# Group 7's second MLP product in seven products of quarters, two slices behind, with its activations' sums on GpSimd

## The chip, the cores and the metric

The kernel runs on one core of one Trainium2 chip. The metric is the device time of one execution in microseconds; lower is better. The kernel before takes 924.25 us (median of three runs, 924.24 to 924.6).

The engines are TensorE (PE; PEld is its weight load), VectorE (DVE), ScalarE (ACT), GpSimd (POOL) and SyncE (SP, which here issues DMAs). Each serves its own list of instructions and waits for the others by semaphores.

## What is computed

Two steps, one after the other. Windowed causal attention with a linear bias over 8 batches of 8 heads, 576 positions, head dimension 64; then a SiLU MLP over the 4608 tokens of width 512, with 2048 hidden features:

```python
scores = where(0 <= i - j < 128, q @ k.T / 8 - slope[h] * (i - j), -1e9)
x = softmax(scores) @ v                       # 4608 tokens x 512
h = x @ w_in                                  # 4608 x 2048
out = (h / (1 + exp(-h))) @ w_out             # 4608 x 512
```

## The kernel before

The tokens are worked through in nine groups of 512 (`NG`, group 0 to 8). A group's MLP is made in 16 slices (`NF`); slice n = 16 g + f has a first product (`gemm1`), an activation in four steps and a second product (`gemm2`). While group g's MLP runs, the attention of group g + 1 is worked through beside it, one pair p (a block of 128 queries, half of the heads) every eight positions of a plan.

**Numbers.** From group 2 on, the operands of the MLP are float16 in two parts, high and low. A product of two such operands is three matmuls: high by high, high by low, low by high.

**Ordinary groups.** `gemm1` makes 12 matmuls of 512 columns into one PSUM bank (tag "h", two banks). `act1` (ACT, L752) is the Tanh of it, `act2` (DVE, L761) turns this into the activation, `act3` (ACT, L778) makes its high part `gh`, `act4` (DVE, L795) its low part `gl`. `gemm2` (L908) makes 12 matmuls of 512 columns, three for each of four token tiles, which gather over the 16 slices in the four banks w, x, y, z. `store` (L929) reads them out.

**The groups in `FAST`** (L67), only the last one before. There a slice is 256 tokens by two tiles of features, and a group falls into two units t = 0, 1 of 256 tokens and eight slices each. `gemm1_fast` (L697) makes 24 matmuls of 256 columns. The second product, a 2x2 by 2x2 product of blocks, is made from seven products of sums of blocks (M1 to M7, Strassen's) instead of eight plain ones: 7 x 3 = 21 matmuls of 256 columns in `gemm2_fast` (L825). For that the activation has seven blocks of 128 instead of four; `act_sums` (L769) makes three of them new by sums, two instructions of 256 elements and one of 128. `act3` and `act4` then each take 640 and 256 elements in two instructions. The sums of the weights are made earlier by GpSimd and ACT (`SUM_WORK`, from position 332 on; the group before the last begins at position 448). M1 has bank z, M5 and M2 bank x, M3 and M4 bank w, M7 and M6 bank y. At the end of a unit `join_products` (L878) adds the seven results up: after the first half of the last slice's second product ACT copies bank x into `once` and DVE reads M1; after the second half DVE reads bank w as a whole, M4 and M3 singly, then bank y; `store_fast` (L872) sends the four quarters out. The last slice of all (`LAST`, 143) is made plainly by `gemm2_last` (L851), in four pieces of six matmuls.

**The order of the work** is written out by hand. The loop over groups makes a list `seq` of halves: two of a slice's first product and two of an earlier slice's second product (`behind`). Each entry is a position; `begin()` (L1161) first issues what the plan has for this position, sorted by `rank` (normalize first, then act2, act_sums, act3, act4, then row_max, p_lo and their kind, then the rest), and then the half product is issued; `act1` follows the second half of a first product. `put` sets plan entries by absolute position, `ahead` by distance from the present one. For a pair whose scores are at position n, in the last batches: `hi16` n-10 and n-8 (ACT), `lo16` n-6 and n-5 (DVE), `scores` n (TensorE), `row_max` n+1 (DVE, four times 256 elements), `exps` n+2 and n+3 (ACT, two each), `p_hi` n+3 and n+4 (ACT), `p_lo` and the DMA transposes n+4 and n+5 (DVE, SP), `attend` n+12 (TensorE), `normalize` n+13 (DVE), `x_hi` and `x_lo` n+15 (ACT, DVE). A new block of values adds `v_hi` at n+7, on GpSimd or, when the group at this position is in `FAST`, on ACT (L421), and `v_lo` at n+8 (DVE). Scores and attended values share two PSUM banks tagged "a" in turn.

In ordinary groups, as group 7 was, slice n-1's second product follows slice n's first, and `act3` and `act4` come two positions after `act1`. In the last group the second products skip slices 1 and 9, to be made up in slices 2 and 10, and those of the last three slices come together at the end.

Waits are set by the tiles: a new tile in a ring of buffers waits for the readers of the tile that had its place.

Of the kernel before, what the change touches and what calls it, by code (L numbers as in the profile page):

```python
# [6 lines left out]
F32 = mybir.dt.float32  # L7
# [10 lines left out]
P = 128  # L18
# [45 lines left out]
Q16 = ("w1_2", "w1_3")  # L64
K16 = ("w1_4", "w1_5", "w1_6")
CUT = 2.0**-25
FAST = (NG - 1,)  # L67
HALF_F = NF // 2
SUMS, SUMS_STEP = 332, 14
SUM_TAGS = tuple(f"w1_{k}" for k in range(7, 15))  # L70
MORE_TAGS = (("w1_15", 1), ("k", KSLOTS), ("k", KSLOTS))
# [25 lines left out]
def tile_window_attention_then_silu_mlp(ctx, tc, qk, qk16, v, w_in, w_out, distance, out):  # L97
# [60 lines left out]
    def ps_of(tag, name):  # L158
        t = psum.tile([P, DM], F32, tag=tag, bufs=2 if tag in "ah" else 1, name=name)
        if tag == "a":  # L160
            spare["a"] = t
        return t
# [615 lines left out]
    def act3(n):  # L778
        gt = gact[n]
        if n // NF in FAST:  # L780
            gh, gl = (pool.tile([P, 7, P], F16, tag=tag, name=f"{tag}{n}") for tag in ("gh", "gl"))
            gact[n] = (gh, gl, gt)
            for to, of in parts_of(n):
                nc.scalar.activation(gh[:, to], gt[:, of], AF.Copy, scale=0.5 * CUT)
            return
        dt = F32R if n // NF < OUT16 else F16
        gh = pool.tile([P, TG], dt, tag="gh", name=f"gh{n}")
        gl = pool.tile([P, TG], dt, tag="gl", name=f"gl{n}")
        if n // NF < OUT16:
            (nc.vector.tensor_copy if at_edge(n) else nc.scalar.copy)(gh, gt)  # L790
        else:
            nc.scalar.activation(gh, gt, AF.Copy, scale=CUT)  # L792
        gact[n] = (gh, gl, gt)
# [31 lines left out]
    def gemm2_fast(n, half):  # L825
        g, (t, j) = n // NF, divmod(n % NF, HALF_F)
        last = LAST - 1 if n // HALF_F == LAST // HALF_F else n - j + HALF_F - 1
        if n == LAST:
            gemm2_last(half)
            return  # L830
        gh, gl, _ = gact[n]
        products = (M5, M2, M1, M3) if half == 0 else (M4, M7, M6)
        for a, parts in ((gh, (0, 1)), (gl, (0,))):
            for k in products:
                b, side = PLACE[k]
                if j == 0 and side == 0 and a is gh:
                    ops[b] = psum.tile([P, DM], F32, tag="wxyz"[b], name=f"m{g}_{t}_{b}")
                for part in parts:
                    nc.tensor.matmul(  # L839
                        product(k), a[:, k], sum_part(k, j, part),  # L840
                        start=j == 0 and side == 0 and a is gh and part == 0, stop=n == last and a is gl,
                        skip_group_check=True,
                    )
        if n == last:
            join_products(g, t, half)

    def product(k):
        b, side = PLACE[k]
        return ops[b][:, side * (DM // 2) : (side + 1) * (DM // 2)]

    def gemm2_last(half):  # L851

        gh, gl, _ = gact[LAST]
        if half == 0:
            ops["c"] = ps_of("a", "last")
        c = ops["c"][:, half * (DM // 2) : (half + 1) * (DM // 2)]
        for col, o in ((0, product(M7)), (1, c)) if half == 0 else ((0, c), (1, product(M6))):
            seq = [
                (a[:, k], w16[1, HALF_F - 1 + far * HALF_F][:, part, col * (DM // 2) : (col + 1) * (DM // 2)])
                for k, far in ((2 + half, 0), (half, 1)) for a, part in ((gh, 0), (gh, 1), (gl, 0))  # L860
            ]
            for i, (lhs, rhs) in enumerate(seq):
                nc.tensor.matmul(
                    o, lhs, rhs, start=half == 0 and col == 1 and i == 0, stop=i == len(seq) - 1, skip_group_check=True
                )
            add_product(o, st["out"][0 if half == col else 1][:, half], NG - 1)
            store_fast(NG - 1, 1, half, col)

    def add_product(m, o, g):
        nc.vector.scalar_tensor_tensor(out=o, in0=m, scalar=gsc[g][:, 2:3], in1=o, op0=ALU.mult, op1=ALU.add)  # L870

    def store_fast(g, t, row, col):  # L872

        first = g * TG + (2 * t + row) * P
        rows = out[first : first + P, col * (DM // 2) : (col + 1) * (DM // 2)]
        (nc.scalar if row and col else nc.sync).dma_start(rows, st["out"][0 if row == col else 1][:, row])

    def join_products(g, t, half):  # L878

        scale = gsc[g][:, 2:3]  # L880
        if half == 0:
            st["out"] = [pool.tile([P, 2, DM // 2], F32, tag="q", bufs=2, name=f"of{g}_{t}_{k}") for k in range(2)]
            st["once"] = once = pool.tile([P, 2, DM // 2], F32, tag="io", name=f"once{g}_{t}")
            nc.scalar.activation(once.rearrange("p a c -> p (a c)"), ops[1], AF.Copy, scale=scale)
            for k in range(2):
                nc.vector.scalar_tensor_tensor(
                    out=st["out"][0][:, k], in0=product(M1), scalar=scale, in1=once[:, k], op0=ALU.mult, op1=ALU.subtract
                )
            return
        (corner, other), once = st["out"], st["once"]  # L890
        nc.vector.scalar_tensor_tensor(
            out=other, in0=ops[0].rearrange("p (a c) -> p a c", a=2), scalar=scale, in1=once, op0=ALU.mult, op1=ALU.add
        )
        for k, m in enumerate((M4, M3)):
            add_product(product(m), corner[:, k], g)
        if n_last(g, t):
            return
        nc.vector.scalar_tensor_tensor(
            out=corner, in0=ops[2].rearrange("p (a c) -> p a c", a=2), scalar=scale, in1=corner, op0=ALU.mult, op1=ALU.add
        )  # L900
        for row in range(2):
            for col in range(2):
                store_fast(g, t, row, col)

    def n_last(g, t):
        return g == NG - 1 and t == 1
# [130 lines left out]
    def put(point, fn, *a):  # L1037
        plan.setdefault(max(point, at(0)), []).append((fn, a))
# [78 lines left out]
    for g in range(1, NG):  # L1117
        put(max(8, at(2 * GT * g) + 10), x_unit, g)
        if g >= IN16:
            put(g * SLICE * NF - 2, mlp_scales, g)  # L1120
    for b in range(1, NBB):

        n = at(2 * GT * (NBLK * b // GT)) + 2
# [14 lines left out]
    def ahead(n, fn, *a):  # L1138
        plan.setdefault(pos[0] + n, []).insert(0, (fn, a))
# [26 lines left out]
    with tc.manual_schedule():  # L1166
# [37 lines left out]
            pos[0] += 1  # L1204
        bank.update(scores=[("a", "a")])

        for g in range(NG):
            now[0] = g

            seq = []  # L1210
            for f in range(NF):
                n = g * NF + f
                behind = [n - 1] if f or g - 1 in FAST else []
                if g in FAST and f in (1, 2, HALF_F + 1, HALF_F + 2):
                    behind = [] if f % HALF_F == 1 else [n - 2, n - 1]
                if g == NG - 1 and f >= NF - 2:
                    behind = [] if f == NF - 2 else [n - 2, n - 1, n]
                elif f == NF - 1 and g not in FAST:
                    behind += [n]
                seq += [("g1", n, 0), ("g1", n, 1)]  # L1220
                seq += [("g2", k, half) for k in behind for half in range(2)]
            for k, n, half in seq:
                begin()
                x_send()
                if k == "g1":
                    gemm1(n, half)
                    if half == 1:
                        act1(n)
                        if n % NF == NF - 1:
                            turn_over(n)  # L1230
                        elif n // NF in FAST and n // NF < NG - 1:
                            ahead(4, act4, n)
                            ahead(3, act3, n)
                            ahead(1, act_sums, n)
                            ahead(1, act2, n)
                        else:
                            late = 1 if n == 0 else 2
                            ahead(3 if 0 < n < NF else late, act4, n)
                            ahead(late, act3, n)
                            ahead(1, act2, n)  # L1240
                else:
                    gemm2(n, half)
                    if n % NF == NF - 1 and n // NF not in FAST:
                        store(g, 2 * half)
                        store(g, 2 * half + 1)
                if g == 0 and (pos[0] in TAKE or pos[0] > TAKE[-1] and pos[0] % 2 == 0):
                    w_next()
                pos[0] += 1
# [41 lines left out]
```

## Time and profile before

| | us |
|---|---|
| median of three runs | 924.25 |
| profiled execution, its own time | 924.52 |
| its span, first to last instruction | 922.7 |
| first Tanh of group 7 | 747.0 |
| first Tanh of group 8 | 840.5 |
| TensorE busy in the span | 910.3 |
| VectorE busy in the span | 697.9 |
| ScalarE busy in the span | 579.0 |
| GpSimd busy in the span | 203.9 |

The profile is of one execution, taken by the hardware profiler. Lines such as L732 are lines of the kernel above. A row of the grouped view has line, engine, operation, what is written and read, shape, count, then busy time and mean duration in ns, then the engine's idle time before these instructions and what ended it. A row of the timeline has start, duration, engine, line, operation, names, shape and how many instructions are merged in it; in brackets the idle time before it and its releaser. A row of the stages has the stretch, its length, the busy times of PE, PEld, DVE, ACT and POOL with counts, the granted TensorE clock and the DMA's share. TensorE's matmuls are pipelined, their ends are modelled, and GpSimd's spans are rough; the spacing of starts is firmer than a duration.

### The profile page before, as it was taken

What the parts mean: (1) busy time and instruction counts of PE and PEld (TensorE: products, weight loads), DVE (VectorE), ACT (ScalarE), POOL (GpSimd) and SP (SyncE); (2) the same over time, 40 slices, a digit from 0 to 9 for tenths busy, and PEclk for the clock granted to TensorE, in tenths of its full rate; (3) what the DMA queues carried; (4) which work ended last, traced back from release to release, by engine and by line L of the source; (5) the groups of instructions that cost most, each with busy time, mean ns of one, the idle gap of its engine ahead of it and who ended that gap; (6) DMA issues with size and microseconds to landing.
All of it is one profiled execution on the core that took longest, in us unless ns stands there. A gap on an engine that the chain in (4) does not pass through costs nothing.

```text
span 922.7 us, 17992 instructions
## 1 busy us (share of the span) xinstructions
PE 910.3 (99%) x6765; PEld 604.5 (66%) x6765; DVE 697.9 (76%) x1704; ACT 579.0 (63%) x1195; POOL 203.9 (22%) x195
## 2 busy tenths in 40 slices
PE   9999999999999999999999999999999999999997
PEld 7867777777787887555555555545455555547886
DVE  6889876446777778898788879888888876645665
ACT  7778997675456764666677756666766665533332
POOL 2343442222221220000000003455655200000000
PEclk9999999999999999999999999999999999999999
DMA  8977825243376645434698736444554464311000
GB/s 303 402 184 223 255 60 134 69 92 73 77 214 155 173 123 136 105 100 104 118 250 209 212 95 160 115 104 104 160 114 108 113 161 103 78 35 59 1 24 23
DMA packets 198182, 122.94 MB, mean 133 GB/s; under 512 B 166480, under 2 KB 167632, under 8 KB 198096
## 3 DMA queue, kind: packets, MB, share of 16 engines
q1 hardware_dynamic: 197664, 121.41, 49.9%
q8 instruction: 53, 0.87, 0.4%
q10 hardware_dynamic: 432, 0.39, 0.2%
q14 instruction: 33, 0.27, 0.1%
HBM read 71.96 MB, written 9.44 MB: 88 GB/s over the span
## 4 chain that ended last, share of the span: by engine, by line
PE 82%; DVE 6%; ACT 2%; issue 1%; ACTq 0%; DVEq 0%
PE o L924 33%; PE h L732 24%; PE h L737 8%; PE av L554 4%; PE h L704 4%; PE sp L450 3%; PE m L839 3%; PE sp L457 2%; DVE gt L763 1%; DVE hr L504 1%; DVE t L480 0%; ACT t L490 0%; DVE w L1021 0%; DVE vmx L209 0%; ACT gt L759 0%
## 5 line engine op out<-in xcount | busy, mean ns | idle before, releaser
L924 PE MATMUL o<-w,gh 128*128 128x512 f16 (+1 forms) x1024 | 313.2, 387 | 0.0
L732 PE MATMUL h<-xt,w 128*128 128x512 f16 (+1 forms) x1344 | 266.7, 349 | 0.0
L924 PE MATMUL o<-w,gl 128*128 128x512 f16 (+1 forms) x512 | 197.3, 385 | 0.3 <-DVE gl L147 0.2
L759 ACT ACTIVATE gt<-h,gsc 128x512 f32<-128x512 f32 x112 | 76.9, 686 | 186.1 <-PE h L732 164.6
L732 PEld LDWEIGHTS <-w 128*128 128x128 f16 x1344 | 125.7, 98 | 103.2 <-issue 2.2
L763 DVE SCALAR_TENSOR_TENSOR gt<-gt,h 128x512 f32<-128x512 f32 x144 | 98.4, 683 | 89.3 <-ACT gt L759 88.3
L490 ACT ACTIVATE t<-t,mx 128x256 f32<-128x256 f32 (+1 forms) x288 | 125.8, 486 | 6.0 <-DVE mx L480 5.7
L504 DVE SCALAR_TENSOR_TENSOR hr<-t,hr 128x512 f16<-128x512 f32 (+1 forms) x128 | 96.7, 761 | 30.1 <-ACT hr L499 30.0
L924 PEld LDWEIGHTS <-gh 128*128 128x128 f16 x640 | 62.1, 98 | 74.3 <-ACT gh L792 0.3
L737 PE MATMUL h<-xh,w 128*128 128x512 f32 x256 | 89.8, 405 | 0.0
L426 POOL TENSOR_SCALAR v<-rv,vsc 128x512 f16<-128x512 f32 x30 | 27.5, 917 | 277.2 <-DMA rv<-v 204.2
L804 DVE SCALAR_TENSOR_TENSOR gl<-gt,gh 128x512 f16<-128x512 f32 x80 | 62.0, 775 | 33.8 <-ACT gh L792 32.7
L924 PEld LDWEIGHTS o<-w,gh 128*128 128x128 f32 x384 | 69.8, 188 | 15.3 <-DVE vsc L269 0.3
L145 POOL TENSOR_TENSOR gl<-gt,gh 128x512 fp32r<-128x512 f32 x30 | 38.6, 1286 | 164.1 <-ACT gh L790 148.8
L499 ACT ACTIVATE hr<-t 128x512 f16<-128x512 f32 (+1 forms) x128 | 71.7, 595 | 1.4 <-DVE hr L504 1.4
L792 ACT ACTIVATE gh<-gt 128x512 f16<-128x512 f32 x80 | 50.3, 629 | 25.3 <-DVE gt L763 22.6
L554 PEld LDWEIGHTS <-hl 128*128 128x128 f16 x1464 | 51.4, 98 | 16.5 <-issue 5.2
L480 DVE CUSTOM_DVE_ANT_0 t<-sp,tab,vsc 128x256 f32<-128x256 f32 (+1 forms) x144 | 58.5, 460 | 1.1 <-PE sp L450 0.7
L924 PEld LDWEIGHTS <-gl 128*128 128x128 f16 x320 | 31.3, 98 | 38.6 <-DVE gl L804 1.0
L554 PE MATMUL av<-v,hl 128*128 128x65 f16 (+1 forms) x1464 | 54.8, 193 | 1.6 <-DVE mx L480 1.5
L145 POOL TENSOR_TENSOR w<-wm,w 128x512 fp32r<-128x512 f32 x32 | 43.4, 1358 | 58.6 <-ACT w L981 58.3
L737 PEld LDWEIGHTS h<-xh,w 128*128 128x128 f32 x256 | 48.1, 188 | 12.2 <-issue 0.2
(173 smaller groups left out, 1357.4 us busy)
## 6 DMA issues: line engine op xcount, KB each, us to landing
r<-qk SPq DMA_DIRECT2D x36, 512.0 KB, 4.0
qs<-qk SPq DMA_DIRECT2D x18, 512.0 KB, 5.1
wr<-w_in SPq DMA_DIRECT2D x16, 512.0 KB, 6.6
wr<-w_out SPq DMA_DIRECT2D x16, 512.0 KB, 6.3
out<-ot SPq DMA_DIRECT2D x32, 256.0 KB, 2.5
rv<-v SPq DMA_DIRECT2D x30, 256.0 KB, 3.9
vm<-v SPq DMA_DIRECT2D x27, 256.0 KB, 5.6
q<-qk SPq DMA_DIRECT2D x18, 256.0 KB, 3.6
```

Of the source, the lines that this page charges most:

```text
L145: engine.tensor_sub(out, a, b)
L480: nc.vector.tensor_tensor_reduce(out=st[p]["t"][u][:, h, 2 * P - n :], in0=st[p]["sp"][h][:, u, o].rearrange("p o c -> p (o c)"), in1=tab[ ...
L490: nc.scalar.activation(x, x, AF.Exp, bias=st[p]["mx"][:, 2 * u + h : 2 * u + h + 1], scale=-1.0)
L499: nc.scalar.activation(split_of(p, u, hr)[:, 0], t[:, :, 2 * P - n :], AF.Copy, scale=PSCALE)
L504: nc.vector.scalar_tensor_tensor(out=hr[:, 1], in0=t[:, :, 2 * P - n :], scalar=PSCALE, in1=hr[:, 0], op0=ALU.mult, op1=ALU.subtract)
L554: nc.tensor.matmul(av[:, 2 * u + h, : rhs.shape[-1]], lhs, rhs, start=(n == 0), stop=(n == len(seq) - 1), skip_group_check=True,)
L732: nc.tensor.matmul(o, w[:, wp, cc], x, start=start and k == 0, stop=stop, skip_group_check=True)
L737: nc.tensor.matmul(hps[n], w[:, cc], x, start=(half == 0 and i == 0), stop=(half == 1 and i == len(seq) - 1), skip_group_check=True,)
L759: nc.scalar.activation(gt, hps[n], AF.Tanh, scale=scale)
L763: nc.vector.scalar_tensor_tensor(out=gt, in0=gt, scalar=1.0, in1=hps[n], op0=ALU.add, op1=ALU.mult)
L804: nc.vector.scalar_tensor_tensor(out=gl, in0=gt, scalar=CUT, in1=gh, op0=ALU.mult, op1=ALU.subtract)
L924: nc.tensor.matmul(ops[ti], a[:, t], w, start=(f == 0 and i == 0), stop=(f == NF - 1 and i == len(seq) - 1), skip_group_check=True,)
```

## The change

Group 7 joins the groups in `FAST`. Second products there run two slices behind the first (`LAG`), over the group's end: slices 126 and 127 of group 7 have theirs in slices 0 and 1 of group 8. So the first two slices of group 7 have no second product, and group 8 skips none. The activations' sums of group 7 are GpSimd's (that branch stood in `act_sums` already), and `act3` and `act4` come four and five positions after `act1` (three and four in the group's first slice). `gh` and `gl` of odd slices take the buffers tagged "gt" and "io", so that four slices have theirs. `once` moves from "io" to "rv". Quarters that are ready are stored ahead of the last addition, all by SP but for the upper row of the last unit, which ACT's queue stores. In `gemm2_last` M7 and M6 are finished first, one addition takes both from their bank, and the two plain pieces have a bank each. The scales of group 8 are made at position 504 instead of 510.

```diff
-FAST = (NG - 1,)
+FAST = (NG - 2, NG - 1)
 HALF_F = NF // 2
+LAG = 2
...
-            gh, gl = (pool.tile([P, 7, P], F16, tag=tag, name=f"{tag}{n}") for tag in ("gh", "gl"))
+            gh, gl = (pool.tile([P, 7, P], F16, tag=tag, name=f"{tag}{n}") for tag in (("gh", "gl"), ("gt", "io"))[n % 2])
...
-        if half == 0:
-            ops["c"] = ps_of("a", "last")
-        c = ops["c"][:, half * (DM // 2) : (half + 1) * (DM // 2)]
-        for col, o in ((0, product(M7)), (1, c)) if half == 0 else ((0, c), (1, product(M6))):
+        for row in range(2):
+            col = row if half == 0 else 1 - row
+            o = product((M7, M6)[row]) if half == 0 else ps_of("a", f"last{row}")[:, : DM // 2]
             seq = [
                 (a[:, k], w16[1, HALF_F - 1 + far * HALF_F][:, part, col * (DM // 2) : (col + 1) * (DM // 2)])
-                for k, far in ((2 + half, 0), (half, 1)) for a, part in ((gh, 0), (gh, 1), (gl, 0))
+                for k, far in ((2 + row, 0), (row, 1)) for a, part in ((gh, 0), (gh, 1), (gl, 0))
             ]
...
-            add_product(o, st["out"][0 if half == col else 1][:, half], NG - 1)
-            store_fast(NG - 1, 1, half, col)
+            if half == 1:
+                add_product(o, st["out"][1][:, row], NG - 1)
+                store_fast(NG - 1, 1, row, col)
+        if half == 0:
+            add_corners(NG - 1, 1)
+
+    def add_corners(g, t):
+
+        corner = st["out"][0]
+        nc.vector.scalar_tensor_tensor(
+            out=corner, in0=ops[2].rearrange("p (a c) -> p a c", a=2), scalar=gsc[g][:, 2:3], in1=corner,
+            op0=ALU.mult, op1=ALU.add,
+        )
+        for row in range(2):
+            store_fast(g, t, row, row)
...
-        (nc.scalar if row and col else nc.sync).dma_start(rows, st["out"][0 if row == col else 1][:, row])
+        (nc.scalar if n_last(g, t) and not row else nc.sync).dma_start(rows, st["out"][0 if row == col else 1][:, row])
...
-            st["once"] = once = pool.tile([P, 2, DM // 2], F32, tag="io", name=f"once{g}_{t}")
+            st["once"] = once = pool.tile([P, 2, DM // 2], F32, tag="rv", bufs=2, name=f"once{g}_{t}")
...
-            put(g * SLICE * NF - 2, mlp_scales, g)
+            put(g * SLICE * NF - (8 if g - 1 in FAST else 2), mlp_scales, g)
...
+        waiting = []
         for g in range(NG):
...
-                behind = [n - 1] if f or g - 1 in FAST else []
-                if g in FAST and f in (1, 2, HALF_F + 1, HALF_F + 2):
-                    behind = [] if f % HALF_F == 1 else [n - 2, n - 1]
-                if g == NG - 1 and f >= NF - 2:
-                    behind = [] if f == NF - 2 else [n - 2, n - 1, n]
-                elif f == NF - 1 and g not in FAST:
-                    behind += [n]
+                waiting.append(n)
+                left = LAG if g in FAST else 1
+                if f == NF - 1 and (g not in FAST or g == NG - 1):
+                    left = 0
                 seq += [("g1", n, 0), ("g1", n, 1)]
-                seq += [("g2", k, half) for k in behind for half in range(2)]
+                while len(waiting) > left:
+                    k = waiting.pop(0)
+                    seq += [("g2", k, 0), ("g2", k, 1)]
...
-                            ahead(4, act4, n)
-                            ahead(3, act3, n)
+                            late = 4 if n % NF else 3
+                            ahead(late + 1, act4, n)
+                            ahead(late, act3, n)
                             ahead(1, act_sums, n)
                             ahead(1, act2, n)
```

More of the change, by code (lines that the diff above doesn't have):

```diff
@@ L830, in gemm2_fast @@
             return
-        gh, gl, _ = gact[n]
+        gh, gl, _ = gact.pop(n) if half else gact[n]
         products = (M5, M2, M1, M3) if half == 0 else (M4, M7, M6)
@@ L863, in gemm2_last @@
                 nc.tensor.matmul(
-                    o, lhs, rhs, start=half == 0 and col == 1 and i == 0, stop=i == len(seq) - 1, skip_group_check=True
+                    o, lhs, rhs, start=half == 1 and i == 0, stop=i == len(seq) - 1, skip_group_check=True
                 )
-            add_product(o, st["out"][0 if half == col else 1][:, half], NG - 1)
-            store_fast(NG - 1, 1, half, col)
+            if half == 1:
[11 more added lines that the diff above has]
+            store_fast(g, t, row, row)
     def add_product(m, o, g):
@@ L895, in join_products @@
             add_product(product(m), corner[:, k], g)
[L896 to L903, printed above, removed]
+        if not n_last(g, t):
+            for row in range(2):
+                store_fast(g, t, row, 1 - row)
+            add_corners(g, t)
     def n_last(g, t):
```

## The prediction

> **What bounds the kernel now.** I read the page, then the stages of the last two groups, then the chain of work in order of time, then TensorE's waits in these groups.
>
> ```profile
> span 922.7 us, 17992 instructions
> PE 910.3 (99%) x6765; PEld 604.5 (66%) x6765; DVE 697.9 (76%) x1704; ACT 579.0 (63%) x1195; POOL 203.9 (22%) x195
> ```
> ```profile
> 651.10:747.00 95.90, 95.78 (x703) 50.12 (x701) 81.80 (x179) 62.83 (x123) 42.36 (x41) 1.00 0.51 123
> 747.00:840.50 93.50, 93.50 (x663) 49.12 (x661) 57.35 (x138) 45.68 (x86) 2.43 (x3) 1.00 0.40 101
> 840.50:915.00 74.50, 73.58 (x675) 65.57 (x673) 47.72 (x99) 28.19 (x49) 0.00 (x0) 1.00 0.03 8
> ```
> The columns of the second fence are PE, PEld, DVE, ACT and POOL, granted clock and DMA. Rows are groups 6, 7 and 8 by time. In group 7 TensorE is never idle, at a full clock, with DVE busy 57 of 93.5 us and GpSimd nearly free. TensorE is the bound there, so time goes only where it works less; and time comes back if another engine's order makes it wait.
>
> ```profile
> 765.77 2.59 PE h L732 x12
> ...
> 850.27 2.62 PE h L704 x24
> 855.18 2.62 PE h L704 x24
> ```
> These are the chain's rows. Group 7's slice has 12 products of 512 columns for each MLP product: 2.59 twice, 5.18. Group 8's slice, already made the new way, repeats after 855.18 - 850.27 = 4.91: 24 of 256 columns in 2.62, so 21 in 2.29.
>
> ```profile
> PE last L863 <- DVE of L870: 1.4, 1, 1.4
> PE m L839 <- ACT gh L784: 0.9, 1, 0.9
> ```
> That is all TensorE waits for after 740 us.
>
> **What it removes.** Group 7's 16 slices shorten by 5.18 - 4.91 = 0.27 each: 4.3 us. In group 8 the 0.9 us wait for `gh` goes:
> ```profile
> 884.84 0.69 ACT L759 ACTIVATE gt<-h,gsc 128x512 f32<-128x512 f32 x1 [3.69 <-DVE of L898]
> ```
> This act1 stood 3.7 us behind a store in ACT's queue (`row and col` on nc.scalar, L876); now only the last unit stores from ACT, and two slices of lag leave `gh` time. In gemm2_last the 1.4 us wait goes: the plain pieces get a PSUM bank each, M7 and M6 are read together by add_corners while TensorE works in other banks, and DVE has one operation of 512 columns for two of 256. The last store leaves as much earlier. Together 6.6 us.
>
> **What it adds in group 7.** Attention of group 8 is worked through meanwhile: one pair of heads' scores per two slices. Before:
>
> ```profile
> 762.49 0.69 ACT L759 ACTIVATE gt<-h,gsc 128x512 f32<-128x512 f32 x1 [3.08 <-PE h L732]
> ...
> 774.47 0.69 ACT L759 ACTIVATE gt<-h,gsc 128x512 f32<-128x512 f32 x1 [3.08 <-PE h L732]
> ```
> Two slices and a pair take 11.98 us, and act1 (Tanh) sits idle 3 us for TensorE. TensorE would need 11.98 - 0.54 = 11.44 after the change. The question is whether ACT, DVE and GpSimd, each serving its queue in program order, can follow.
>
> First, the order. Slices 0 and 1 of group 7 now have no second product, so from slice 2 on the plan's positions come two earlier in the slices. `scores` of a pair (position n) stood ahead of the odd slice's first product; now it stands behind it, so row_max (n+1) queues on DVE behind act2 and act4, which come after act1 of that slice. exps (n+2, n+3) and p_hi (n+3) then lie on ACT ahead of act1 of the even slice, and act3 (four positions after act1) with them. In the even slice act2, the sums on GpSimd, act3 and x_hi lie ahead of the next odd slice's act1. This closes a loop that does not pass through TensorE: act2 (odd), act4, row_max, exps, act3, exps, p_hi, act1 (even), act2, act4, p_lo, last sum, act3, x_hi, act1 (odd).
>
> Its steps. By lines in 747:840.5:
> ```profile
> L759 ACT ACTIVATE gt<-h,gsc 128x512 f32<-128x512 f32 x16 | 11.0, 689 | 40.1 <-PE h L732 40.1
> L490 ACT ACTIVATE t<-t,mx 128x256 f32<-128x256 f32 x24 | 10.7, 495 | 0.0
> L792 ACT ACTIVATE gh<-gt 128x512 f16<-128x512 f32 x16 | 10.1, 630 | 4.6 <-DVE gt L763 3.8
> L499 ACT ACTIVATE hr<-t 128x512 f16<-128x512 f32 x12 | 6.8, 614 | 0.0
> ...
> L591 ACT CAST x<-xs 128x256 f16<-128x256 f32 x7 | 2.7, 388 | 0.0
> ```
> ```profile
> L763 DVE SCALAR_TENSOR_TENSOR gt<-gt,h 128x512 f32<-128x512 f32 x16 | 11.0, 687 | 23.1 <-ACT gt L759 23.1
> L480 DVE CUSTOM_DVE_ANT_0 t<-sp,tab,vsc 128x256 f32<-128x256 f32 x24 | 10.2, 479 | 0.5 <-PE sp L450 0.5
> L504 DVE SCALAR_TENSOR_TENSOR hr<-t,hr 128x512 f16<-128x512 f32 x12 | 8.2, 682 | 0.6 <-ACT hr L499 0.6
> ```
> Count and busy time give the steps: act1 0.69, a pair of exps 0.89, p_hi 0.57, x_hi 0.39, act2 0.69, three of the four row_max 1.28 (the first exps need three), p_lo 0.68. act3 and act4 grow to 640 + 256 elements; group 8 shows them, and its sums on DVE:
> ```profile
> 854.43 0.42 DVE L774 TENSOR_TENSOR gt<-gt 128x256 f32<-128x256 f32 x1
> ...
> 855.55 1.04 ACT L784 ACTIVATE gh<-gt 128x640 f16<-128x640 f32 x2 [1.88 <-DVE gt L776]
> 856.32 1.16 DVE L799 SCALAR_TENSOR_TENSOR gl<-gt,gh 128x640 f16<-128x640 f32 x2 [0.80 <-ACT gh L784]
> ```
> act3 1.04, act4 1.16, sums 1.12 where DVE makes them. On GpSimd the sums are two operations of 256 elements and one of 128, and they meet act4 and p_lo. What meeting costs shows in group 6, DVE first, then GpSimd:
> ```profile
> 671.11 1.21 DVE L399 SCALAR_TENSOR_TENSOR k<-r,vsc,k 128x512 f16<-128x512 f32 x1
> 672.24 1.21 DVE L504 SCALAR_TENSOR_TENSOR hr<-t,hr 128x512 f16<-128x512 f32 x1
> ```
> ```profile
> 668.77 0.73 POOL L663 TENSOR_TENSOR wq<-wr 128x256 f32<-128x256 f32 x1
> ...
> 671.74 1.17 POOL L667 TENSOR_TENSOR wq<-wr 128x256 f32<-128x256 f32 x1
> ```
> They take turns: DVE steps by 1.13 where such an operation takes 0.68 undisturbed, GpSimd needs 1.17 for 0.73. Operations that read PSUM (row_max, act2) keep their length. So act4 is 1.16 + 0.5 for the turn of one sum = 1.66, p_lo 1.13. No row shows a sum of 128 elements; it lies between 0.3 (the DVE one) and 0.73; I take 0.45.
>
> Odd half: 0.69 + 1.66 + 1.28 + 0.89 + 1.04 + 0.89 + 0.57 + 0.69 = 7.7. Even half: 0.69 + 1.66 + 1.13 + 0.45 + 1.04 + 0.39 + 0.69 = 6.05. The loop is 13.8; every second pair has v_lo (1.13, on DVE ahead of row_max) and v_hi (moved from GpSimd to ACT; 0.57, as p_hi of the same size): 15.5. Mean 14.6 against TensorE's 11.44: 3.2 late per pair. Nor can TensorE run far ahead:
> ```profile
> L554 PE MATMUL av<-v,hl 128*128 128x65 f16 (+1 forms) x1464 | 54.8, 193 | 1.6 <-DVE mx L480 1.5
> ...
> L457 PE MATMUL sp<-k,q 64*128 64x128 f32 x544 | 41.9, 286 | 2.6 <-DVE xs L581 1.1 <-PE h L737 0.9 <-DMA k<-qk 0.3
> ```
> With two PSUM banks tagged "a", attend waits for row_max of the next pair and scores for normalize of the last but one; both have happened. Five pairs (67 to 71) make 16. When scores have ended, TensorE asks for an odd slice's `gl` 11.44 + 0.87 (eight products with `gh`) - 1.0 (act1 and its start) = 11.3 after that slice's act2, and the loop gives its first piece after 7.7 + 0.69 + 0.8 = 9.2: the last 2 us of lateness are free. The dense start (three first products of slices 0 to 2 in a row, with two scores' work) makes DVE late by about as much, an estimate; the two cancel. Neighbours on one engine overlap by up to 0.1 at some ten places of five loops, so I take 14.5; with both ends of the sums' price and of the meetings (0.3 to 0.7 each), 6 to 20.
>
> [...] With the sums on DVE instead (1.12 each, no turns) the halves would be 8.3 and at least 3.9, 12.2 and more a pair: late as well, so the sum would shrink by up to 1.5 a pair and keep its sign.
>
> **Smaller terms.** Between the last product of a unit and the next unit there is now one first product instead of two, in group 8's first and second unit:
> ```profile
> 877.29 0.60 PE L839 MATMUL m<-w,gh 128*128 128x256 f16 x4
> ...
> 882.62 0.87 DVE L870 SCALAR_TENSOR_TENSOR of<-m,gsc,of 128x256 f32<-128x256 f32 x2
> ```
> M3 of the new unit needs its bank at 877.29 + 4.91 + 0.65 (six products) = 882.85, DVE leaves it at 883.49: 0.65 twice. At the seam turn_over(127) puts act4(127), which waits for GpSimd, ahead of act4(126) on DVE: act1 0.95 (with its start), act2 0.69, sums 1.9, act3's first piece 0.77, act4(127) 1.16 and the first piece of act4(126) 0.8 make 6.3; `gl` is wanted after 2.29 + 2.62 + 0.87 = 5.8: 0.5, and handovers make it 0.7. Together 2. SP's stores wait for DVE ahead of a pair's transposes, which DVE releases later anyway: nothing. gsc's move, "rv" for `once` and the tags: nothing, the last reader is long done.
>
> **Sum.** The profiled execution took 924.5 (span 922.7): 924.5 - 6.6 + 14.5 + 2.0 = 934.4. The runs' median is 0.3 lower: 934.1, say 934. With 6 to 20: 925.6 to 939.6.
>
> **Rivals.**
> - *TensorE stays the bound (faster).* If the sums fall into DVE's gaps, act4 stays 1.16 and p_lo 0.68, the sums end 1.9 after act2, and the even half shrinks to act2, sums, act3, x_hi, act1: 4.7; the odd half is 7.2. That is 11.9, with v 13.2: 1.1 over per pair, 5 in all, which overlapping neighbours and the free 2 us take up. Then 924.25 - 6.6 + 2 = 919.7. It decides if act4 in group 7 shows 1.2 and not 1.7. For it: GpSimd is busy 42 of 96 us in group 6 and TensorE hardly waits there. Against: the order there leaves row_max ahead of act1.
> - *The lateness is paid once.* Loop nearer 12.5, swallowed by two slices of lag until the unit turns in slice 10, where joins stand behind all DVE has queued: 2 to 6 there. 924.25 - 6.6 + 2 + 4 = 923.7.
>
> **Numbers.** Slower by the loop 0.70; paid once 0.10; faster 0.20. 0.2%, 1.8 us, is about what a measurement of this kernel can tell from no change; so faster 0.20, same 0.10, slower 0.70. The slower case alone spans 925.6 to 939.6; to leave out no more than 2 in 10 the range reaches to the faster case's middle: 919.5 to 939.5.
>
> **What would show it.** In group 7: ACT's act1 no longer waits for TensorE; TensorE idles over 10 us, for row_max ahead of `attend` and for normalize ahead of `scores`; L799 lasts 1.5 or more; two slices take over 13 us. I am wrong if TensorE is busy throughout group 7 and a pair of slices takes 11.4 there: then the loop failed at the meetings or at the order of the queues. Tail: no wait at L863; group 8: waits of 0.6 at its units' first M3.

## The result, and the profile after

The changed kernel takes 935.5 us (median of four runs, 935.03 to 937.17) against 924.29 for the kernel before (four runs as well): 1.0124 times as long, with a 95% interval of 1.0112 to 1.0136. The forecast was 934.0. The profiled execution is the longest of the four, 937.17 us; its span is 12.5 us longer than that of before. The page's first lines:

```profile
span 935.2 us, 18766 instructions
...
PE 911.4 (97%) x7101; PEld 639.7 (68%) x7101; DVE 720.9 (77%) x1730; ACT 586.8 (63%) x1214; POOL 244.1 (26%) x240
```

TensorE is busy for about as long as before (910.3), in a longer span. The stages, from the first Tanh of group 7 to that of group 8, and from there to the last Tanh (PE, PEld, DVE, ACT, POOL, clock, DMA):

```profile
747.10:847.40 100.30, 88.53 (x949) 78.05 (x946) 77.25 (x157) 52.53 (x105) 42.42 (x48) 0.98 0.35 87
847.40:924.10 76.70, 75.06 (x670) 66.27 (x671) 50.12 (x104) 27.28 (x47) 0.00 (x0) 0.98 0.05 15
```

Group 7 begins where it did, at 747, and lasts 100.3 us instead of 93.5, although two of its second products have moved into group 8's time. TensorE, never idle there before, now misses 12 us, and the clock is no longer 1.00. What TensorE waits for after 740 us (total, times, longest):

```profile
PE sp L451 <- DVE xs L582: 6.6, 4, 2.0
PE m L840 <- DVE gl L800: 2.7, 1, 2.7
PE av L555 <- DVE mx L481: 2.7, 3, 1.5
PE m L840 <- DVE of L883: 1.0, 2, 0.5
PE av L555 <- DMA hl<-hr: 0.3, 1, 0.3
```

13.3 us in eleven waits, where there were two of 0.9 and 1.4. Most stand ahead of `scores`, for normalize, and ahead of `attend`, for row_max: the two places that the loop of the prediction named. The act1 rows say the same from the other side:

```profile
761.38 0.67 ACT L760 ACTIVATE gt<-h,gsc 128x512 f32<-128x512 f32 x1
769.42 0.67 ACT L760 ACTIVATE gt<-h,gsc 128x512 f32<-128x512 f32 x1
775.12 0.68 ACT L760 ACTIVATE gt<-h,gsc 128x512 f32<-128x512 f32 x1
```

None of them has a bracket. Act1, which stood idle 3 us for TensorE, follows other ACT work at once, and two slices take 13.74 us (761.38 to 775.12), not 11.98. One turn of the loop in the timeline (start, duration, engine, line), with act2, act4, sums, row_max, exps and act3 of an odd slice, then act1 and the even slice as far as `scores`:

```profile
775.83 0.69 DVE L764 SCALAR_TENSOR_TENSOR gt<-gt,h 128x512 f32<-128x512 f32 x1 [0.16 <-ACT gt L760]
...
776.44 1.68 DVE L800 SCALAR_TENSOR_TENSOR gl<-gt,gh 128x640 f16<-128x640 f32 x2
...
776.60 1.24 POOL L775 TENSOR_TENSOR gt<-gt 128x256 f32<-128x256 f32 x1 [2.75 <-DVE gt L764]
...
778.05 0.47 DVE L481 CUSTOM_DVE_ANT_0 t<-sp,tab,vsc 128x256 f32<-128x256 f32 x1
...
778.56 0.51 ACT L491 ACTIVATE t<-t,mx 128x256 f32<-128x256 f32 x1 [2.15 <-DVE mx L481]
778.79 0.45 POOL L777 TENSOR_TENSOR gt<-gt 128x128 f32<-128x128 f32 x1
...
779.78 1.03 ACT L785 ACTIVATE gt<-gt 128x640 f16<-128x640 f32 x2
...
782.04 0.66 ACT L760 ACTIVATE gt<-h,gsc 128x512 f32<-128x512 f32 x1
...
786.47 0.42 DVE L582 TENSOR_TENSOR xs<-av,r 128x256 f32<-128x256 f32 x1
786.50 1.04 ACT L785 ACTIVATE gh<-gt 128x640 f16<-128x640 f32 x2 [2.67 <-POOL gt L777]
...
786.95 0.95 PE L451 MATMUL sp<-k,q 128*128 128x128 f16 x14 [1.00 <-DVE xs L582]
```

Act4 takes 1.68 us while GpSimd's first sum takes 1.24 beside it; row_max can start only at 778.05, ACT stands 2.15 for it and later 2.67 for GpSimd's last sum, and TensorE at last stands for normalize.

**Where the 12.5 us lie.** Removed: products 4.3, the `gh` wait 0.9, the tail 0.9. Added: waits 13.3, and 1.8 that the pauses last longer than the list says (from start to start they add up to 15.1; the weight loads' row of the longest pause ahead of `scores` has 2.14 where the matmuls' has 1.97). That is 9.0. The last 3.4 are a slow TensorE clock, in two stretches of 3.4 us each at half speed. This adds up TensorE's time; it does not say that the time would be 3.4 us shorter at a full clock (the fifth experiment comes back to it). These are stages cut around both:

```profile
798.00:801.20 3.20, 1.35 (x14) 1.07 (x11) 3.13 (x7) 0.54 (x2) 2.75 (x3) 1.00 0.00 0
801.40:804.70 3.30, 3.30 (x23) 2.75 (x24) 2.77 (x5) 2.00 (x5) 1.12 (x1) 0.50 0.81 165
804.80:806.00 1.20, 1.20 (x13) 1.08 (x12) 0.53 (x2) 0.69 (x1) 1.12 (x3) 1.00 0.53 193
...
849.20:852.50 3.30, 3.30 (x18) 2.38 (x16) 1.98 (x5) 1.04 (x2) 0.00 (x0) 0.50 0.00 0
```

### The profile page after: what moved, and what is told of

Read it like the earlier page. It is cut to its first block, busy times and chain, and to the rows that moved or that the text cites. A ratio compares the mean times of both kernels' runs of the same rounds, so it can differ in the third digit from the quotient of the medians.

```text
span 935.2 us, 18766 instructions
## 1 busy us (share of the span) xinstructions
PE 911.4 (97%) x7101; PEld 639.7 (68%) x7101; DVE 720.9 (77%) x1730; ACT 586.8 (63%) x1214; POOL 244.1 (26%) x240
## 4 chain that ended last, share of the span: by engine, by line
PE 72%; DVE 10%; ACT 5%; POOL 2%; issue 2%; DMA 0%; DVEq 0%; POOLq 0%; ACTq 0%; SPq 0%
PE o L933 28%; PE h L733 20%; PE h L738 8%; PE h L705 4%; PE m L840 4%; PE av L555 4%; PE sp L451 3%; PE sp L458 2%; DVE gt L764 2%; ACT gt L760 1%; DVE t L481 1%; ACT t L491 1%; POOL gt L775 1%; DVE gl L800 1%; DVE hr L505 1%
## 5 line engine op out<-in xcount | busy, mean ns | idle before, releaser
L933 PE MATMUL o<-w,gh 128*128 128x512 f16 (+1 forms) x896 | 275.2, 388 | 0.0
L733 PE MATMUL h<-xt,w 128*128 128x512 f16 (+1 forms) x1152 | 222.6, 344 | 0.0
L933 PE MATMUL o<-w,gl 128*128 128x512 f16 (+1 forms) x448 | 173.1, 386 | 0.3 <-DVE gl L148 0.2
L733 PEld LDWEIGHTS <-w 128*128 128x128 f16 x1152 | 107.7, 98 | 83.5 <-issue 2.2
L505 DVE SCALAR_TENSOR_TENSOR hr<-t,hr 128x512 f16<-128x512 f32 (+1 forms) x128 | 100.1, 788 | 29.7 <-ACT hr L500 29.6
L705 PE MATMUL h<-xt,w 128*128 128x256 f16 x768 | 90.2, 275 | 0.0
L933 PEld LDWEIGHTS <-gh 128*128 128x128 f16 x512 | 49.7, 98 | 59.2 <-ACT gh L793 0.3
L705 PEld LDWEIGHTS <-w 128*128 128x128 f16 x768 | 75.9, 99 | 9.6
L427 POOL TENSOR_SCALAR v<-rv,vsc 128x512 f16<-128x512 f32 x27 | 25.3, 936 | 213.6 <-DMA rv<-v 164.1
L805 DVE SCALAR_TENSOR_TENSOR gl<-gt,gh 128x512 f16<-128x512 f32 x64 | 51.2, 800 | 25.9 <-ACT gh L793 25.0
```

The lines of the kernel that those rows point to most:

```text
L505: nc.vector.scalar_tensor_tensor(out=hr[:, 1], in0=t[:, :, 2 * P - n :], scalar=PSCALE, in1=hr[:, 0], op0=ALU.mult, op1=ALU.subtract)
L705: nc.tensor.matmul(out, w[:, wp, cc], xt[g, "g"][:, 2 * t : 2 * t + 2, xp * NCC + cc], start=half == 0 and i == 0, stop=i == len(seq) - 1, ...
L733: nc.tensor.matmul(o, w[:, wp, cc], x, start=start and k == 0, stop=stop, skip_group_check=True)
L933: nc.tensor.matmul(ops[ti], a[:, t], w, start=(f == 0 and i == 0), stop=(f == NF - 1 and i == len(seq) - 1), skip_group_check=True,)
```

## The experiments

Two theories. **The order** (theory 1): the plan's positions, two earlier in the slices, put `scores` behind the first product and so close a loop through ACT, DVE and GpSimd; it is longer than TensorE's work, and moving the positions or shortening the loop restores the time. **The turns** (theory 2): DVE and GpSimd lengthen each other's operations where they meet (act4 takes 1.68 us beside GpSimd's first sum and 1.16 at 846.11, without it; that sum 1.24 beside act4 and 0.73 at 843.37, with DVE idle), and without their meetings the time is restored, whatever the order. All edits are to the changed kernel. The kernel before had a median of 924.4 to 924.5 beside them.

**Only the last group in `FAST`.** Removed waits, two PSUM banks in the tail and two slices of lag stay; group 7 is ordinary.

```diff
-FAST = (NG - 2, NG - 1)
+FAST = (NG - 1,)
```


> Group 7 is an ordinary group again; group 8 keeps its two slices of lag, the bank for each plain piece and the stores by SP. Both theories agree: group 7 as before (93.5 us from first Tanh to first Tanh), 0.9 us of wait for gh and about 1 us of the tail gone, one wait of some 0.5 us where the second unit starts. 922.5 to 923.5, against 924.3 before. If the edits in the last group had a share in the loss, it would lie above 925.

923.3 us, ratio to before 0.9987 (0.9978 to 0.9996), a little faster than before. TensorE's only wait after 740 us:

```profile
PE m L840 <- DVE of L883: 0.5, 1, 0.5
```

So the whole loss belongs to group 7's new form, its seam to group 8 included. The gain from the rest is 1.1 us.

**The scores two positions earlier**, from pair 66 on, which puts them ahead of the odd slice's first product again.

```diff
-    return STEP * (p - 2 * GT) - LEAD
+    return STEP * (p - 2 * GT) - LEAD - (2 if p >= 2 * GT * (NG - 1) + 2 else 0)
```


> The changed kernel with every plan position of the pairs from 66 on two earlier, so that scores stand ahead of the odd slice's first product again and row_max ahead of act2; the sums stay on GpSimd. Theory 1 (the order of the queues closes a loop through ACT, DVE and GpSimd): the chain between two Tanh falls to DVE's own work, 11 to 11.7 us for two slices; TensorE's waits in group 7 ahead of the seam fall from about 10 us to under 3, and 924 to 928 results (the wait at the seam stays). [...]

926.73, ratio 1.0023 (1.0014 to 1.0032): 8.8 of the 11.2 us come back. Two rows of its timeline:

```profile
775.34 1.69 ACT L491 ACTIVATE t<-t,mx 128x256 f32<-128x256 f32 x4
...
776.08 1.69 DVE L800 SCALAR_TENSOR_TENSOR gl<-gt,gh 128x640 f16<-128x640 f32 x2
```

Act4 lasts as long as in the changed kernel, so the turns are all there. But the four exps follow act1 without a wait, since row_max is done, and two slices take 11.5 us (act1 at 763.26, 774.75, 786.19). The turns alone do not make the lateness: by that theory two slices would still take over 13 us, and the time stay over 932.

**The sums on DVE**, so that nothing takes turns.

```diff
-        engine, a = nc.vector if n // NF == NG - 1 else nc.gpsimd, gact[n]
+        engine, a = nc.vector, gact[n]
```


> The changed kernel with group 7's sums on DVE instead of GpSimd: no turns, but 1.1 us more of DVE's own in the chain. Theory 1: the loop stays, 12.5 to 13.5 us for two slices, 931 to 935. Theory 2: with the turns gone two slices take near 11.5, below 926.

931.28, ratio 1.0076 (1.0063 to 1.009): 4.2 us come back, the seam's wait among them. The waits in the loop stay:

```profile
PE sp L451 <- DVE xs L582: 7.0, 4, 2.0
PE av L555 <- DVE mx L481: 1.5, 3, 1.1
```

Without the sums' meetings the loop is still late: two slices take 13.4 us (act1 at 760.54 and 773.99). So the turns alone are not the cause. What the turns cost is not shown by this run, since DVE has the sums' own time in their place.

**No sums in group 7**, in the changed order: `act_sums` returns at once there and act3 and act4 take as many elements from the four blocks, so what they would have made is left out.

```diff
+        if n // NF < NG - 1:
+            return [(slice(3, 7), slice(0, 4)), (slice(0, 3), slice(1, 4))]
...
+        if n // NF < NG - 1:
+            return
```


> The changed kernel without group 7's three sums: act3 and act4 take as many elements, from copies of the four blocks, so group 7's output lacks the sums. It prices the sums in all. Theory 1: the odd half of the loop shrinks by half a us (act4 without a turn) and the even half by more than 1 us (act3 no longer behind GpSimd); two slices 11.4 to 12, 924 to 927 with the seam's wait smaller. Theory 2: 11.4 and below 924.

920.25, ratio 0.9955 (0.9941 to 0.9968). The theory of the order as I had put it misses this; it is what the theory of the turns gave. Its waits (lines are 4 further on):

```profile
PE m L844 <- DVE of L887: 1.0, 2, 0.5
PE sp L451 <- DVE xs L582: 0.6, 1, 0.6
```

The order is the same, yet two slices take 11.4 us (act1 at 759.15, 770.60, 782.04). I had priced the order alone at some lateness; it has next to none, 0.6 us ahead of `scores`. The sums cost 15 us in this order, the seam and the slow clock included, by act3's wait for them and by what they do to act4 and p_lo. Together with the two runs ahead of it, which kept the sums, this says that the lateness needs both: the order makes the loop, and the sums make it longer than TensorE's work. The figure is also close to what the change would bring without any lateness, as only 1.6 us of waits are left in it.

**The seam.** `turn_over` in group 7's last slice is left out, so act4(126) is first on DVE.

```diff
-                        if n % NF == NF - 1:
+                        if n % NF == NF - 1 and g != NG - 2:
```


> The changed kernel, but slice 127's activation steps keep the distances of the other slices instead of following its Tanh at once, so act4 of slice 126 no longer stands behind act4 of slice 127 on DVE. If that order makes the 2.7 us wait at the seam and the halved clock after it follows from the wait: the wait and some 1.6 us of slow matmuls go, 931 to 932. If the seam's wait is only the loop's lateness arriving there, it stays over 1.5 us, and 933.5 or more.

933.18, ratio 1.0093 (1.008 to 1.0106), between the two expectations. The 2.7 us for `gl` are gone, but the next join waits longer:

```profile
PE sp L451 <- DVE xs L582: 4.8, 3, 2.0
PE m L840 <- DVE of L883: 2.2, 2, 1.6
```

The second row was 1.0 with a longest of 0.5. TensorE, no longer held at the seam, asks for M3's bank before DVE has cleared it, and 1.2 of the 2.7 us is paid there.

This run also shows what a slow clock costs inside the loop. Its profile has a half-speed stretch of 3.41 us from 774.99, where the changed kernel's clock is full. The same two slices, from act1 to act1, in the changed kernel and then here (length, PE, PEld, DVE, ACT, POOL, clock, DMA):

```profile
775.12:788.37 13.25, 12.24 (x140) 11.01 (x137) 10.95 (x23) 8.14 (x18) 5.45 (x6) 1.00 0.42 114
```
```profile
775.06:788.31 13.25, 13.25 (x136) 11.46 (x134) 10.95 (x23) 8.13 (x17) 5.45 (x6) 0.87 0.41 114
```

Both take 13.25 us: with the slow clock TensorE is busy throughout, with the full clock it waits 1.0 us. The four runs of this kernel say the same: 932.78 us at a mean clock of 1.000, 933.27 at 0.999, 933.09 and 933.57 at 0.996.

**Both, with the scores earlier from pair 67 on.**


> The changed kernel with the plan positions of the pairs from 67 on (not 66, which stood ahead of its slice's first product already) two earlier, and slice 127's steps at the other slices' distances. Against 926.7 with the pairs from 66 on: the wait of 1.4 us of scores at the end of group 6 and the 1.8 us at the seam go, 923 to 924.5. If pair 67, now six positions behind 66, pays instead, 925 to 926.

924.62, ratio 1.0005 (0.9996 to 1.0014): level with before and just over what was expected. The eleven runs fall into two heaps, eight at 924.23 to 925.13 with a mean clock of 1.000 and three at 926.44 to 926.74 with 0.998. The profiled execution, 926.44, has one half-speed stretch, from 771.35, and the heaps' medians lie 2.1 us apart: here, where the other engines no longer hold TensorE in every pair, a slow stretch goes with more time.

**The same with the sums on DVE.**


> The same with group 7's sums on DVE. In this order DVE's own work should set the pace: the turns cost DVE about 2.3 us for two slices, the sums themselves 2.2. So the same within 1 us, 922 to 925; if GpSimd's length (act3 behind it), and not DVE's work, is what is left, 920 to 922.

929.29, ratio 1.0049 (1.0037 to 1.006): a miss. With a full clock it takes 927.4 to 927.6 (two runs), 3 us more than with the sums on GpSimd. In the changed order the sums were better on DVE, in this one they are better on GpSimd: here act2, the three sums and act4 stand on DVE ahead of normalize, from 770.09 to 772.9 in the profile, while TensorE waits for it from 771.15 to 773.76.

```profile
PE sp L451 <- DVE xs L582: 5.5, 3, 2.6
```

So one and the same move, from GpSimd to DVE, gained 4.2 us in the changed order, most of it at the seam, and lost 3 in this one.

**One position earlier from pair 62, two from pair 66**, with the seam.

```diff
+    return STEP * (p - 2 * GT) - LEAD - (2 if p >= 66 else 1 if p >= 62 else 0)
```


> As the kernel with scores two positions earlier and slice 127's steps at the other slices' distances, but the step of two positions is spread: pairs 62 to 65 one earlier, from 66 on two. The waits of scores at the start of group 7 (3.0 us when the step came at once, with a halved clock after) fall to 1 or less, the unit's turn stays: 922 to 923.5, level with the kernel that only has the last group's edits (923.3). If the dense first slices of group 7 make that wait, and not the step, 924 to 925.

924.41, ratio 1.0001 (0.9992 to 1.001), a miss by 1 us. The time lies in the second expectation's range, but not for its reason:

```profile
PE m L840 <- DVE of L883: 3.2, 3, 1.7
PE sp L451 <- DVE xs L582: 0.5, 2, 0.3
```

The waits for normalize are gone as meant, and those for the joins at the turn of the units have grown from 2.6 to 3.2. That the joins stand behind all that DVE has queued is my reading; no run tests it.

## Why the prediction was right

The sign and the mechanism held. That the size came out so near is in part luck: the loop was put too high, the seam too low and the clock at nothing, and these made up for each other.

- **Removed, 6.6.** The wait for `gh` is gone, and no wait at L863 is left. The tail gave 0.9 instead of 1.4 us. DVE's rows there stand close:

```profile
930.58 0.75 DVE L875 SCALAR_TENSOR_TENSOR of<-m,gsc,of 128x512 f32<-128x512 f32 x1
931.25 0.87 DVE L883 SCALAR_TENSOR_TENSOR of<-last,gsc,of 128x256 f32<-128x256 f32 x2
```

  The last additions follow one another on DVE, which now sets the end; before, the last one waited 0.17 us for TensorE. Removed in all: 6.1.
- **The loop, 14.5.** Its path and prices hold: act4 1.68 (taken 1.66), p_lo and the last sum together 1.5 (784.95 to 786.46; taken 1.58), v_lo and v_hi 1.7 (taken 1.70), act1 without a wait. Row_max, which reads PSUM, keeps its length beside GpSimd's sums as forecast: 0.47 at 778.05 and 778.45, beside sums at 777.80 and 778.79, where group 7 of before had a mean of 0.48. Too large was the turn itself. From act1 to act1 of the even slices it takes 12.6 us without v_lo and v_hi (769.42 to 782.04) and 14.4 with them (782.04 to 796.40), forecast 13.8 and 15.5. From act2 to act2 the odd half is 6.9 (775.83 to 782.73), not 7.7, and the even half 5.7 (797.10 to 802.82), not 6.05. I let two exps start after three row_max; in the rows the first starts after one, at 778.56, and only one lies between row_max and act3: 0.4 us. The rest is neighbours on ACT and DVE that start up to 0.1 before the one ahead has ended; for this I had taken only 1.5 off all five pairs. The other way went a term that the forecast did not have: a unit turns within group 7, and its joins stretch one pair to 15.6 us (odd act1 at 802.11 and 817.67, with the first slow stretch at its start), where the others take 13.3 to 13.7. The loop's waits came to 9.6; with their restarts, that is their part of the 1.8 us by which pauses outlast the list, 10.9.
- **Smaller terms, 2.0.** The joins wait 0.5 twice where 0.65 was forecast. The seam is the term that was mis-sized: 2.7, not 0.7.

```profile
840.65 1.04 ACT L785 ACTIVATE gh<-gt 128x640 f16<-128x640 f32 x2 [3.47 <-POOL gt L777]
...
841.89 0.68 ACT L760 ACTIVATE gt<-h,gsc 128x512 f32<-128x512 f32 x1
...
846.11 1.16 DVE L800 SCALAR_TENSOR_TENSOR io<-gt,gt 128x640 f16<-128x640 f32 x2 [2.82 <-ACT gt L785]
847.19 1.15 DVE L800 SCALAR_TENSOR_TENSOR gl<-gt,gh 128x640 f16<-128x640 f32 x2
...
848.06 0.39 PE L840 MATMUL m<-w,gl 128*128 128x256 f16 x2 [2.70 <-DVE gl L800]
```

  The mechanism is the forecast one: act4(127), the third row, goes ahead of act4(126), which TensorE wants, and the chain from act1(127) to `gl` takes 6.2 us (841.89 to 848.06), forecast 6.3. But I let it begin with the end of its product, at 839.6, and act1(127) stood behind act3(126), which waits for GpSimd's last sum: 2.3 us late. 6.2 + 2.3 - 5.8 = 2.7.
- **Not forecast: the clock.** As TensorE's time, with restarts, loop 10.9, joins 1.3, seam 3.0 and clock 3.4, less 6.1, make 12.5. The forecast came to 9.9 (16.5 less 6.6). But the first of the two slow stretches lies in the loop, where the fifth experiment shows that a slow clock can cost nothing because TensorE then waits less. So 3.4 is the most that the clock can have cost, and up to 1.7 of it belongs to the loop, which then makes 10.9 to 12.6. No run separates the two, and the four runs of the changed kernel do not follow their clock (935.03 us at 0.996, 935.80 at 0.998). The loop was put 1.9 to 3.6 too high, the seam 2.3 too low, the clock at nothing. Of the 2.6 between forecast and measurement, 1.7 is that this execution is the longest of the four.
- **The rivals.** "TensorE stays the bound" was to be decided by act4 in group 7: it shows 1.68, not 1.2. "Paid once" falls as well: the waits lie in every pair. The case that the prediction weighed, the sums on DVE, was late as well, as it said: the move from GpSimd to DVE shortens five pairs of the loop by only 0.7 us (act1 from 760.54 to 829.88 instead of 761.38 to 831.41). The forecast's bound of up to 1.5 us a pair is far from reached; most of the 4.2 us is the seam's wait of 2.7 and what follows it.

Left open: whether the products' 4.3 us can be had beside attention at all. Each order tried gave the lateness another place (scores, joins, seam). Another place for act3, which waits up to 2.7 us for GpSimd's last sum at the head of ACT's queue, was not tried. Nor was a third bank for scores: each of the kernel's eight PSUM tiles (two each of h and a, then w, x, y, z) has its work here.

## What to carry to other kernels

When a slice gets shorter on the bound engine, write down the loop that the other engines' queues close without it, one row for each step, and compare its length with the new slice: here the new order alone cost next to nothing, the sums with the scores moved back some 4 to 6.5 us (924.4 to 926.7 against 920.25; that order without sums was not run), both together 15. A plan in absolute positions shifts against the work as soon as a lag is added; where `scores` stood before a product and where it stands after was worth 8.8 us, twice the gain of the change. Look at the clock behind each pause of TensorE: six pauses of 2.14 to 2.98 us here had 3.4 us at half speed behind them, 1.7 us of TensorE's work; two of 2.76 and 2.79 had not. In the sixth experiment, where the other engines no longer held it in every pair, such a stretch went with some 2 us (924.5 and 926.65, the medians of the heaps); in the fifth, where it would have waited anyway, with nothing (13.25 us in both).

## What the runs showed of the hardware

**Behind some pauses of TensorE its clock was 0.50 for some 3.4 us (3.41 in the changed kernel), behind others as long it stayed at 1.00.** The profiles of four kernels show six such stretches between 740 us and the last matmul. Start of each, and ahead of it the pause by the weight loads' rows (length, end):

| kernel | half speed from | pause |
|---|---|---|
| changed | 801.35 | 2.14, to 801.32 |
| changed | 849.14 | 2.98, to 848.06 |
| sums on DVE | 800.55 | 2.20, to 800.53 |
| seam | 774.99 | 2.14, to 774.27 |
| seam | 802.30 | 2.14, to 801.26 |
| both | 771.35 | 2.16, to 770.57 |

The length of the pause does not decide alone. The same pause ahead of `scores` in the changed kernel and in the seam's experiment, the changed one first:

```profile
774.33 0.78 PEld L451 LDWEIGHTS <-q 128*128 128x128 f16 x14 [2.14 <-DVE xs L582]
```
```profile
774.27 0.79 PEld L451 LDWEIGHTS <-q 128*128 128x128 f16 x14 [2.14 <-DVE xs L582]
```

In the changed kernel the clock stays at 1.00 behind it, through the two slices above. In the experiment it falls:

```profile
774.50:775.00 0.50, 0.50 (x13) 0.50 (x10) 0.32 (x1) 0.50 (x3) 0.00 (x0) 0.99 0.33 79
775.00:778.00 3.00, 3.00 (x19) 2.20 (x17) 2.65 (x5) 1.35 (x3) 1.46 (x2) 0.50 0.82 179
```

Two longer pauses in the seventh experiment, of 2.76 and 2.79 us to 759.52 and 773.76, have a clock of 1.00 behind them. What decides is not shown.

A stretch of 3.41 us at 0.50 takes 1.7 us of TensorE's work. In the runs of both edits together that shows as time: the two heaps of runs above (924.2 to 925.1 and 926.4 to 926.7, mean clock 1.000 and 0.998) fit one such stretch. In the loop of the seam's experiment it cost nothing, as the 13.25 us above show. This is read from traces; no run moved a pause on purpose.
